# Second-level operand sums loaded one item ahead and a part of them split when formed, in a transformer block on one core

## The chip, the core and the metric

The kernel runs on one core of a Trainium2 chip. The metric is the device time of one execution in microseconds (us); of several runs the median is given. TensorE (PE) multiplies matrices, VectorE (DVE), ScalarE (ACT) and GpSimd (POOL) work elementwise, and SyncE (SP) issues every transfer between HBM and the on-chip memory (SBUF), in order. Each engine takes its instructions in the order of the program and stands at one whose inputs aren't there.

## The reference, cut to what matters

A block of 2048 tokens and width 1024: a normed attention with memory over four segments of 512 tokens, then a gated feed-forward with 3584 hidden columns, in float32.

```python
h = layernorm(x) * (1 + ca) + sa
x = x + ga * attention(h, wq, wk, wv, wo, beta)
h = layernorm(x) * (1 + cb) + sb
x = x + gb * ((gelu(h @ w_gate) * (h @ w_up)) @ w_down)
```

The change lies in the gate and up products `h @ w_gate` and `h @ w_up`, and in the places where this stage begins and ends.

## The kernel before, in words

**Products.** Every operand of the feed-forward's products is split into a high part (rounded, type fp32r) and a low part (the rest). A product is then three matmuls: high by high, low by high, high by low. The high part is a copy on ACT, the low part a subtraction on DVE, or on POOL in pieces of 256 columns.

**Two levels.** Gate and up are computed with a scheme of seven products for a 2 by 2 blocking instead of eight (products 1 to 7; 1 and 2 use the gate weights, 5 and 6 sums and differences of both weights, and 7, 3 and 4 are done later in `gate_up`). Products 1, 2, 5 and 6 are themselves cut by the same scheme a second time, so each has seven products r in the order ROUND = (1, 5, 6, 2, 7, 3, 4). An inner product is six matmuls of 128x128 by 128x512.

**Rounds.** `two(n)` runs for n = 0 to 27 (NJ = 14). Rounds 0 to 13 do products 1 and 2 for two chunks of hidden columns each, rounds 14 to 27 products 5 and 6. In a round the fourteen inner products (r, i) alternate between the two outer products i. After each inner product `ended` empties its PSUM bank (lines 1260 to 1289: ACT copies or DVE additions, L1270, L1274, L1276, L1280), and then `step()` advances every generator in the list `sides` by its rate. One such call is named a step here. `later(k, f)` runs f k steps on; stores are issued so. The bank of product 6 also takes 7 and 4, so 4 can't start until the addition for 7 (L1274) has read it; the bank of product 1 is copied into that bank by ACT first (L1260). y tiles, the results of the second outer product, have three buffers, which the base loads of rounds 14 and later (`base_load`, L1225) share.

**The operand from the tokens.** The activations' sums for products 1 and 2 are made by `a_early` and `a_first` while attention's output projections still run (`projections`, L783). The ones for 5 and 6 are made beside rounds 1 to 12 by `mixes`: first-level sums of the normed activations, eight items of two loads (h2_d to rm tiles, L964), three DVE sums and one POOL difference (L973), four stores to mix_d (L974); then second-level sums, four items of the same form (`a_mix_two`, L1012, to mix2_d). An item's loads stand at its beginning, four steps ahead of its first sum. `mixes` stands after the first four items until segment 3 of the tokens is normed (`norm_steps`, beside rounds 1 to 5). Their tiles have two buffers of each of two kinds (U, ra).

**The two entrances.** In round 13 each operand tile of products 1 and 2 comes free when its last product is done. `a_second` then fills it with the part for 5 or 6: 28 parts (seven r, two i, two halves c), six pairs loaded ahead (L1136, L1140), each split by `put_two` (ACT L1029, low half L933). In round 27 `a_last` does the same for the first-level operands of 7, 3 and 4, twelve loads (L1338) in `todo`, four ahead, each into a U or ra tile and split by `put_a` (ACT L936, low half L933). `gate_up(u)` then uses them; `cg_load` and `gu_load` bring its base sums and weights (L1362, L1368 to L1370). `b_two`, `b_one` and `b_part` prepare the weights' operands beside all of this (BB and B tiles; eight B buffers).

**Order.** All engines' orders in this stage are those of the program text: `manual_schedule` leaves nothing to a planner.

## Time and profile before

| | |
|---|---|
| median of 3 runs | 2688.2 us (2684.89 to 2689.12) |
| the profiled execution | 2689.39 us, span of its instructions 2687.5 us |
| PE busy | 2635.1 us, 98% of the span |
| DVE, ACT, POOL busy | 1742.5, 1382.0, 1043.0 us |
| mean granted TensorE clock | 0.997 |
| DMA | 617.83 MB, mean 230 GB/s |

The rows shown further on come from several views. In a row of the timeline stand the start in us from the span's beginning, the duration, engine, line, operation, output and inputs by the program's names, and the count of merged instructions; in brackets the idle time of the engine just before and what ended it. In a table of stages each row is a stretch of time with every engine's busy us. In a list of waits stand the waiter, whom it waited for, the total in us, how often, and the longest. SPq is the queue in which SP issues transfers. Where a helper records the instruction, its line is the helper's (L933: a sum or difference; L936 and L1029: a rounding copy).

The attention and its projections end at about 1116 us; rounds 0 to 27 of `two` run from there to 1686 us, `gate_up` to about 2166 us, the last product to the end.

### The profile page before, as it was taken

Reading aid. Unit: us, or ns where it says so; the run is one execution under the profiler, and the core shown is the slowest. Engines: PE = TensorE matmul, PEld = TensorE weight load, DVE = VectorE, ACT = ScalarE, POOL = GpSimd, SP = SyncE. Lnnn points to the kernel's source line nnn. Section 1 sums busy time; section 2 is a strip of 40 time slices with the busy share of each in tenths; the row PEclk is TensorE's granted clock in tenths of the full one; section 3 lists DMA queues with packets and bytes.
Section 4 is the critical chain, followed back from the end, with each engine's and each line's share of the span. In section 5 each row is a group of like instructions: output and inputs, shape, how many; then the busy total and the mean of one; then the engine's idle time right before and its main releaser. Section 6 shows DMA issues by size and latency. Waiting matters only on the chain.

```text
span 2687.5 us, 42440 instructions
## 1 busy us (share of the span) xinstructions
PE 2635.1 (98%) x13905; PEld 2188.8 (81%) x13905; DVE 1742.5 (65%) x3685; ACT 1382.0 (51%) x3163; POOL 1043.0 (39%) x1578
## 2 busy tenths in 40 slices
PE   7999999999999999999998999999999999999999
PEld 6788888888888788777876888788888888888887
DVE  7676656776676745776776555676767554574456
ACT  6778767776767724565564434433333333243323
POOL 4233334433333532334566675487877200000000
PEclk9999999999999999999999999999999999999999
DMA  7355444534443567487897778999999896885563
GB/s 266 107 156 159 112 140 134 153 103 138 138 128 101 169 207 263 143 292 265 306 315 266 276 270 289 345 363 375 360 359 365 302 325 222 274 296 196 189 207 123
DMA packets 284253, 617.83 MB, mean 230 GB/s; under 512 B 29056, under 2 KB 53632, under 8 KB 284032
## 3 DMA queue, kind: packets, MB, share of 16 engines
q1 hardware_dynamic: 284032, 615.13, 68.0%
q8 instruction: 109, 1.79, 0.3%
q14 instruction: 112, 0.92, 0.1%
HBM read 378.56 MB, written 186.12 MB: 210 GB/s over the span
## 4 chain that ended last, share of the span: by engine, by line
PE 88%; DMA 5%; DVE 4%; ACT 2%; issue 2%; POOL 0%; SPq 0%; DVEq 0%; ACTq 0%; POOLq 0%
PE y L1669 19%; PE f L1468 16%; PE kv L405 9%; PE pb L1248 6%; PE q L411 6%; PE y L783 6%; PE pa L1248 4%; PE pc L1248 4%; PE S L617 3%; PE T L705 3%; PE O L717 3%; PE kT L524 2%; PE vT L524 2%; DMA rm<-h_d 1%; PE num L673 1%
## 5 line engine op out<-in xcount | busy, mean ns | idle before, releaser
L1669 PE MATMUL y<-B,L 128*128 128x512 f32 x2352 | 533.8, 389 | 0.9 <-ACT L L936 0.6
L1669 PEld LDWEIGHTS y<-B,L 128*128 128x128 f32 x2352 | 441.4, 188 | 93.2 <-ACT L L936 1.0
L1468 PE MATMUL f<-A,B 128*128 128x512 f32 x2016 | 459.4, 390 | 3.9 <-ACT A L936 3.4
L1468 PEld LDWEIGHTS f<-A,B 128*128 128x128 f32 x2016 | 379.1, 188 | 84.0 <-ACT A L936 3.8
L621 ACT ACTIVATE sj<-sj,mm 128x384 f32<-128x384 f32 (+3 forms) x512 | 281.1, 552 | 39.9 <-DVE mm L619 39.4
L708 POOL TENSOR_SCALAR_AFFINE_SELECT pt<-pt 128x128 f32<-128x128 f32 x512 | 166.1, 346 | 332.6 <-ACT pt L707 324.5
L619 DVE CUSTOM_DVE_ANT_0 sj<-S,mask 128x384 f32<-128x384 f32 (+3 forms) x512 | 228.3, 488 | 96.5 <-PE S L617 70.2
L1248 PE MATMUL pb<-AA,BB 128*128 128x512 f32 x1008 | 250.8, 395 | 15.2 <-DVE AA L933 4.9
L707 ACT ACTIVATE pt<-T 128x256 f32<-128x256 f32 (+3 forms) x512 | 182.3, 443 | 132.3 <-PE T L705 126.0
L1248 PEld LDWEIGHTS pb<-AA,BB 128*128 128x128 f32 x1008 | 188.2, 189 | 63.0 <-DVE AA L933 8.1
L936 ACT ACTIVATE L<-X 128x512 fp32r<-128x512 f32 x168 | 105.7, 629 | 256.1 <-PE y L1669 165.4
L933 DVE TENSOR_TENSOR L<-X,L 128x512 fp32r<-128x512 f32 x168 | 115.9, 691 | 144.6 <-ACT L L936 144.5
L396 POOL TENSOR_TENSOR w<-r,w 128x256 fp32r<-128x256 f32 x180 | 133.8, 776 | 141.2 <-ACT w L390 141.2
L1495 ACT ACTIVATE g<-f 128x512 f32<-128x512 f32 x56 | 33.5, 598 | 285.0 <-PE f L1468 285.0
L405 PE MATMUL kv<-w,hha 128*128 128x256 f32 x896 | 173.8, 285 | 2.2 <-DVE vx L423 2.2
L1248 PE MATMUL pc<-AA,BB 128*128 128x512 f32 x672 | 163.3, 390 | 2.1 <-DVE AA L933 2.1
L1248 PE MATMUL pa<-AA,BB 128*128 128x512 f32 x672 | 164.0, 393 | 0.0
L1248 PEld LDWEIGHTS pc<-AA,BB 128*128 128x128 f32 x672 | 125.5, 188 | 30.0 <-DVE AA L933 3.9
L1248 PEld LDWEIGHTS pa<-AA,BB 128*128 128x128 f32 x672 | 127.4, 190 | 27.3 <-issue 0.5
L405 PEld LDWEIGHTS kv<-w,hha 128*128 128x128 f32 x896 | 143.9, 191 | 3.4 <-DVE vx L423 2.5
L933 DVE TENSOR_TENSOR BB<-t_a,BB 128x512 fp32r<-128x512 f32 x98 | 78.6, 802 | 86.3 <-ACT BB L936 86.2
L933 POOL TENSOR_TENSOR t_a<-g,t_a 128x256 f32<-128x256 f32 x112 | 95.6, 874 | 89.0 <-DVE BB L933 83.7
(295 smaller groups left out, 5442.4 us busy)
## 6 DMA issues: line engine op xcount, KB each, us to landing
B<-wc_d SPq DMA_DIRECT2D x112, 512.0 KB, 3.5
cg<-st_d SPq DMA_DIRECT2D x168, 256.0 KB, 6.3
st_d<-x SPq DMA_DIRECT2D x112, 256.0 KB, 2.7
st_d<-y SPq DMA_DIRECT2D x112, 256.0 KB, 3.1
hid_d<-g SPq DMA_DIRECT2D x56, 512.0 KB, 6.0
wc_d<-T SPq DMA_DIRECT2D x56, 512.0 KB, 4.6
X<-hid_d SPq DMA_DIRECT2D x112, 256.0 KB, 4.8
wr<-gd_d SPq DMA_DIRECT2D x84, 256.0 KB, 4.0
```

Source lines behind the costliest of these rows:

```text
L396: nc.gpsimd.tensor_sub(w[:, 1, c], r[:, c], f32(w[:, 0, c]))
L405: nc.tensor.matmul(ps, b[:, sl], w[:, a], start=(kt == 0 and a == 0 and b is hi), stop=(kt == KT - 1 and a == 1), **kw)
L411: nc.tensor.matmul(ps, w[:, a], b, start=(kt == 0 and a == 0 and b is hi), stop=(kt == KT - 1 and a == 1), **kw)
L619: nc.vector.tensor_tensor_reduce(out=sj[:, :nv], in0=ps[:, :nv], in1=mask[:, L - nv:], scale=-1.0, scalar=3.4e38, op0=ALU.add, op1=ALU.min ...
L621: nc.scalar.activation(sj[:, :nv], sj[:, :nv], AF.Exp, bias=mm[:, j, i:i + 1], scale=-1.0, accum_out=ll[:, i, j:j + 1])
L707: nc.scalar.activation(pt, ps[:, nn - n:nn], AF.Exp)
L708: nc.gpsimd.affine_select(pt[:, :P], pt[:, :P], pattern=[[1, P]], compare_op=ALU.is_ge, fill=0.0, base=0, channel_multiplier=-1)
L783: nc.tensor.matmul(ps, b[:, i * P:(i + 1) * P], w[:, a, g % 2], start=(g == 0 and a == 0 and b is hi), stop=(g == G - 1 and a == 1))
L933: f(*xs)
L1248: nc.tensor.matmul(ps, w[:, a, at:at + P], A["a", i, r, k][b], start=(r in (1, 5) and k == a == b == 0), stop=(k == 1 and a == 1), skip_gr ...
L1468: nc.tensor.matmul(ps, B[fc, i][:, a, kt * P:(kt + 1) * P], A[p, i, kt][b], start=False, stop=(kt == 3 and a == 1), skip_group_check=True)
L1669: nc.tensor.matmul(banks[t], ops[k][:, y, t * P:(t + 1) * P], B[slots[k]][:, x], start=(i not in (2, 4, 3) and j == 0 and x == 0 and y == ...
```

## The change

- `mixes` is one list of twelve items, each loaded one item ahead: at the end of the item before for the first five (and then eight steps before its first sum), behind the first sum of the item before for the others. Items alternate between U and ra tiles from the fifth on. First-level items form their sums in the order r = 5, 7, 6, 3 (before 5, 6, 7, 3), the one for 6 in place of an input.
- In the four second-level items, the parts for r = 5 and 7 (8 of the 28) are split at once: two ACT copies and two DVE subtractions, then stored as high and low to a new array hl_d (16 stores of 256 KB, in place of 8). `a_second` loads them straight into the operand tiles (16 loads of 256 KB) and splits only the other 20; two of these low halves (r = 6, c = 1) go to POOL.
- `base_load(14, 1)` stands behind product (2, 7) of round 13 instead of (2, 6).
- `a_last`: the last two of its twelve loads go into B tiles, issued in round 27 behind product (5, 7). `gu_load(2)` moves from the first to the second unit of `gate_up`.
- Before round 0, four parts of `a_first` are issued ahead of the five filling matmuls, and then one part a step instead of two. `a_first` forms one difference of each sum on POOL instead of DVE.
- `norm_steps`: segment 3 waits one step more before its transposes; segment 2 takes statistics and scaling one call earlier, the transposes one later (two calls a step there).

```diff
-                for _ in range(4):
+                for _ in range(5):
                     yield
                 turn(q, 0)
...
-        period, at_stat, at_scale, at_turn = (5, 5, 7, 10) if len(toks) > 4 else (4, 6, 8, 13)
+        period, at_stat, at_scale, at_turn = (5, 5, 7, 10) if len(toks) > 4 else (4, 5, 7, 14)
...
+            def one(p, kt):
                 r = []
                 for k in (kt, kt + 4):
-                    t = ra_tile(f"rm{p}_{k}") if p and kt % 2 else flat(pair_tile(f"rm{p}_{k}", "U"))
-                    nc.sync.dma_start(t, h2_d[k * P:(k + 1) * P, tok:tok + PASS])
+                    t = ra_tile(f"rm{p}_{k}") if p and kt % 2 == 0 else flat(pair_tile(f"rm{p}_{k}", "U"))
+                    nc.sync.dma_start(t, h2_d[k * P:(k + 1) * P, p * PASS:(p + 1) * PASS])
                     r.append(t)
...
+            items = [(one, p, kt) for p in range(2) for kt in range(4)] + [(two, i, c) for c in range(2) for i in PAIRS[1]]
+            homes = {0: items[0][0](*items[0][1:])}
...
+            for n, (f, x, y) in enumerate(items):
+                a11, a12, a21, a22 = homes[n]
+                if n < 5:
+                    for _ in range(8):
+                        yield
+                s1, s3 = c_tile(f"m1_{n}"), c_tile(f"m3_{n}")
+                split = f is two
+                for r, t, g, p_, q_ in ((5, s1, nc.vector.tensor_add, a21, a22), (7, s3, diff, a11, a21),
+                                        (6, a11, nc.vector.tensor_sub, s1, a11), (3, a12, nc.vector.tensor_sub, a12, a11)):
+                    g(t, p_, q_)
+                    k = (MIX.index(r) * 2 + y) * P
+                    if not split:
+                        later(3, lambda r=r, t=t, x=x, y=y: nc.sync.dma_start(mix_rows(x, r)[y * P:(y + 1) * P], t))
+                    elif r in (6, 3):
+                        later(3, lambda t=t, k=k, x=x: nc.sync.dma_start(mix2_d[x - 5][k:k + P], t))
                     yield
+                    if r == 5 and n > 3:
+                        ahead(n)
+                    elif r != 5 and (r != 6 or not split):
                         yield
+                if split:
+                    for r, t, h in ((5, s1, a22), (7, s3, a21)):
+                        nc.scalar.activation(h.bitcast(F32R), t, AF.Copy)
+                    yield
+                    for r, t, h in ((5, s1, a22), (7, s3, a21)):
+                        nc.vector.tensor_sub(t.bitcast(F32R), t, h)
+                        for q, src in enumerate((h, t)):
+                            k = (4 * (r == 7) + 2 * y + q) * P
+                            later(2, lambda src=src, k=k, x=x: nc.sync.dma_start(hl_d[x - 5][k:k + P], src))
+                        yield
+                else:
+                    yield
+                if n < 4:
+                    while n == 3 and not normed(3):
+                        yield
+                    ahead(n)
...
-                nc.vector.tensor_sub(s3, a11, a21)
+                diff(s3, a11, a21)
...
+                if r in (5, 7):
+                    for c in range(2):
+                        n = 8 * ROUND.index(r) + 4 * (i in (2, 6)) + 2 * c
+                        hl = A["a", i, r, c] = [a_tile(n + q, f"AA{i}_{r}_{c}_{q}") for q in range(2)]
+                        for q in range(2):
+                            k = (4 * (r == 7) + 2 * c + q) * P
+                            nc.sync.dma_start(f32(hl[q]), hl_d[i - 5][k:k + P])
+                    yield
+                    continue
                 for c in range(2):
-                    put_two(i, r, c, rs[q][c], nc.vector)
-                    if q and not c:
+                    put_two(i, r, c, rs[r, i][c], nc.gpsimd if r == 6 and c else nc.vector)
+                    if began and not c:
                         load()
...
-                if (second or n == NJ - 1) and (i, r) == (other, 6) and n + 1 < 2 * NJ:
+                if (i, r) == ((other, 6) if second else (other, 7)) and NJ - 1 <= n < 2 * NJ - 1:
                     base_load(n + 1, 1)
+                if n == 2 * NJ - 1 and (i, r) == (one, 7):
+                    ff["rest"]()
...
-                    t = (ra_tile if q % 4 > 1 else lambda n: pair_tile(n, "U"))(f"ra{p}_{i}_{b}")
+                    get = b_tile if q > 9 else ra_tile if q % 4 > 1 else lambda n: pair_tile(n, "U")
+                    t = f32(get(f"ra{p}_{i}_{b}"))
...
+            ff["rest"] = lambda: [load(q) for q in (10, 11)]
...
+        for _ in range(4):
+            next(ff["first"])
+        for e in sides:
+            if e[0] is ff["first"]:
+                e[1] = 1
         for q in range(5):
             nc.tensor.matmul(s_ps(f"full{q}"), B["a", 0, 1][:, 0, :P], A["a", 1, 1, 0][0], start=True, stop=True)
...
-                if fc + 2 < FC:
+                if 0 < fc < FC - 2:
                     gu_load(fc + 2)
+            if u == 1:
+                gu_load(2)
```

79 lines of the change are left out of this document (28 added, 51 removed).

## The prediction

> **What bounds the kernel now.** I read the page first, then the table of stages, then the list of who waited for whom, and last single rows at the gaps. The page says what can be won at all:
>
> ```profile
> span 2687.5 us, 42440 instructions
> PE 2635.1 (98%) x13905; PEld 2188.8 (81%) x13905; DVE 1742.5 (65%) x3685; ACT 1382.0 (51%) x3163; POOL 1043.0 (39%) x1578
> ```
>
> TensorE idles 52.4 us. The change adds and removes no matmul, so it can only touch this idle time and the clock. The table of stages (length, then busy us of PE, PEld, DVE, ACT, POOL, then granted clock, DMA share, GB/s) says where it lies:
>
> ```profile
> 0.00:100.00 100.00, 78.66 (x497) 67.24 (x498) 68.96 (x192) 67.28 (x135) 39.94 (x76) 0.97 0.62 211
> 1060.00:1116.00 56.00, 54.15 (x253) 44.12 (x252) 41.09 (x81) 21.25 (x39) 6.84 (x8) 1.00 0.51 165
> 1116.00:1140.00 24.00, 22.06 (x90) 17.76 (x89) 15.03 (x21) 14.22 (x25) 12.30 (x15) 0.93 0.32 110
> 1140.00:1303.00 163.00, 155.84 (x692) 125.74 (x691) 115.57 (x178) 92.19 (x171) 75.91 (x85) 1.00 0.83 279
> 1384.00:1437.00 53.00, 43.10 (x165) 30.23 (x164) 43.01 (x58) 31.76 (x61) 32.02 (x33) 0.98 0.89 318
> 1437.00:1686.00 249.00, 249.00 (x1094) 205.41 (x1093) 140.75 (x204) 102.31 (x180) 153.00 (x188) 1.00 0.78 277
> 1686.00:1708.00 22.00, 18.11 (x71) 13.90 (x70) 16.24 (x24) 11.80 (x21) 4.05 (x4) 0.92 1.05 405
> ```
>
> The opening's 21.3 us stay: nothing before 1060 us is edited. Five stages are in reach, by length less PE busy: end of the projections 1.85, round n=0 1.94, the rounds with the second-level sums (n=1 to 9) 7.16, the change from products 1 and 2 to 5 and 6 (n=13, 14) 9.90, the entrance to gate and up 3.89. Sum 24.7 us. A step (one product of six matmuls) is 249 / 1094 x 6 = 1.37 us, a round 19.1 us.
>
> Two of the gaps' groups (who waited for whom: us in total, times, longest) are needed below:
>
> ```profile
> PE tpb L269 <- ACT nb L248: 1.9, 2, 1.3
> PE tpc L269 <- ACT nc L248: 1.6, 2, 0.9
> ```
>
> The clock belongs to it. These rows show matmuls right behind a gap; the last number in brackets is PE's idle time:
>
> ```profile
> 1127.18 2.86 PE L1248 MATMUL pb<-AA,BB 128*128 128x512 f32 x6 [1.94 <-DVE x L1274]
> ...
> 1244.72 1.66 PE L1248 MATMUL pb<-AA,BB 128*128 128x512 f32 x6 [2.78 <-DVE y L1274]
> ...
> 1434.59 1.22 PE L1248 MATMUL pb<-AA,BB 128*128 128x512 f32 x2 [2.34 <-DVE AA L933]
> 1435.61 3.99 PE L1248 MATMUL pa<-AA,BB 128*128 128x512 f32 x12
> ...
> 1703.71 0.50 PE L1468 MATMUL f<-A,B 128*128 128x512 f32 x1 [3.38 <-ACT A L936]
> ```
>
> Six matmuls take 2.86 us at 1127 and 1.66 at 1244. The stages' clocks of 0.93 over 24 us and 0.92 over 22 us are 1.7 us of lost work each; the 14 matmuls from 1434.59 on end at 1439.60, 5.0 us instead of 14 x 0.228 = 3.2 and a tail, so I count 1.7 there too. So three gaps cost 5.1 us beyond their length, and the longer gap at 1244 cost nothing: length alone doesn't decide. The Trainium skill ("TensorE: Matmul & The Clock Gate", "What's actually happening") has the clock halve after an idle window of about 3.4 us, and the window runs free. The trace disagrees on the threshold: 1.94 and 2.34 us were enough. By the page only the third gap's 1.7 us would come back.
>
> In reach altogether: 24.7 + 5.1 = 29.8 us.
>
> **Part 1, end of the projections (1.85 us).** The transposes of segment 2 wait for the scaled rows: tpb's 1.9 us in two waits. Statistics and scaling move half a step up, the turn half a step down: 1.37 us more distance. I leave 0.3; gain 1.5 (0 to 1.9). The later turn delays the first sums by 0.7 us; the differences that go from DVE to POOL there are hidden, since POOL is busy 6.84 of those 56 us. If they weren't, DVE would wait for one pair of POOL instructions, 1.8 us by the 75.91 us that 85 of them take at 1140.
>
> **Part 2, round n=0 (1.94 + 1.7).** ACT's and DVE's rows:
>
> ```profile
> 1118.47 0.58 ACT L1260 ACTIVATE pb<-pa 128x512 f32<-128x512 f32 x1 [4.81 <-PE pa L1248]
> 1118.96 1.14 ACT L1029 ACTIVATE AA<-u 128x512 fp32r<-128x512 f32 x2
> ```
>
> ```profile
> 1119.62 1.29 DVE L933 TENSOR_TENSOR AA<-u,AA 128x512 fp32r<-128x512 f32 x2 [2.95 <-ACT AA L1029]
> 1126.45 0.69 DVE L1274 TENSOR_TENSOR x<-pb,x 128x512 f32<-128x512 f32 x1
> ```
>
> ACT stands 4.81 us at a bank copy that needs the first product, the splits queue behind it, DVE idles 2.95 us for them, and PE later waits 1.94 us for DVE's addition at 1126.45. Four parts issued ahead of the first product run in that hole: 4 x 0.57 = 2.3 us of ACT inside 4.81, and DVE's 2.95 us exceed the 1.94 missing. One part a step instead of two also puts fewer subtractions ahead of the addition. Gain 3.4 (0, if those tiles' memory comes free only with the last projection, to 3.6).
>
> **Part 3, sums one item ahead (7.16).** DVE's waits of these rounds, two of the seven rows, and the DMA issues (KB, median us to landing):
>
> ```profile
> DVE m L973 <- DMA rm<-h_d: 28.7, 7, 6.3
> ```
>
> ```profile
> 1150.82 0.69 DVE L973 TENSOR_TENSOR m<-rm,rm 128x512 f32<-128x512 f32 x1 [4.22 <-DMA rm<-h_d]
> ...
> 1242.77 0.69 DVE L973 TENSOR_TENSOR m<-rm,rm 128x512 f32<-128x512 f32 x1 [5.54 <-DMA rm<-h_d]
> ```
>
> ```profile
> rm<-h_d SPq DMA_DIRECT2D x16, 512.0 KB, 6.9
> mix_d<-rm SPq DMA_DIRECT2D x15, 256.0 KB, 5.3
> ```
>
> The load stands four steps (5.5 us) ahead of its first sum and lands in 6.9 us or more; DVE stands still, and the additions that empty PSUM queue behind it. The wait of 4.22 has no gap behind it, that of 5.54 the 2.78 at 1244. Of the 7.16 us, 1.6 are tpc, the transposes of segment 3, which get one step more (1.37 us against 0.9 at most); the other 5.5 are such additions that came late.
>
> The lead becomes eight steps for the first five items, seven or eight after: 9.6 to 10.9 us. But the tiles limit it: nine of the twelve loads enter a tile whose last store is issued in the same step or one before, and SP stands until that store lands, with the st_d stores and weight loads queued behind. Store 5.3 plus load 6.9 is 12.2 us, so waits of 1.3 to 2.6 us remain, below the 4.22 that cost nothing. DVE's third sum now follows POOL's difference by two steps, 2.7 us against two POOL instructions; a POOL that comes late would hold DVE there. The four split items add two ACT copies and two DVE subtractions each, into stages where ACT is busy 57% and DVE 71%.
>
> What grows is DMA. An eight-step item moves 2.1 MB in 10.9 us (192 GB/s), a nine-step split item 2.6 MB in 12.3 us (213), and a round's weights and st_d stores are 3.15 MB in 19.1 us (165): 357 to 378 GB/s. This stage's 279 GB/s at share 0.83 make 336 at full share; 405 were reached at 1686. So by the end the backlog lies between nothing and 33 us x 21 and 49 us x 42 GB/s, 2.8 MB or 8 us. I take half of that, which brings the last two items back to waits of 5 us and gaps near 1.5: 3.2 left, gain 4.0 (-3 to 7.2).
>
> **Part 4, n=13 and 14 (9.90 + 1.7).**
>
> ```profile
> L933 DVE TENSOR_TENSOR AA<-w,AA 128x512 fp32r<-128x512 f32 x28 | 23.0, 846 | 0.3 <-ACT AA L1029 0.3
> L1029 ACT ACTIVATE AA<-w 128x512 fp32r<-128x512 f32 x28 | 16.9, 622 | 0.0
> ```
>
> ```profile
> 1397.54 0.69 DVE L1280 TENSOR_TENSOR y<-pa,x 128x512 f32<-128x512 f32 x1 [3.25 <-DMA st_d<-y]
> ```
>
> DVE is the bound: 43.0 of 53.0 us busy, 10 in waits. PE needs 43.1 less 1.7 of slow clock, 41.4. The change takes 8 low halves off DVE and moves 2 to POOL: 10 x 0.846 = 8.5 us; 8 x 0.622 = 5.0 off ACT. The 3.25 us wait is for a y tile whose store hadn't landed: the base load ahead of it took the older tile. Moved four products down, it takes the younger one, and the wait goes. The sums also end earlier, since they no longer stand until segment 3 is normed, so the first six operand loads (3 MB) leave n=13. DVE then needs 53.0 - 8.5 - 3.2 = 41.3 against PE's 41.4, a tie, in which the order still costs something: I leave 3.5, gain 8.1 (3 to 11.6). Late next are the sixteen 256 KB loads straight into operand tiles. Those of r=7 are issued in n=14's first two steps and needed eight steps (10.9 us) on; a load of these rounds that meets DMA at its fullest stage lands in some 7 (the 6.9 above). If they were 3 us late, PE would wait 3; the range holds that.
>
> POOL's share of this is doubtful. Such an instruction on DVE takes 0.69 us at 1242.77 and 0.846 in the mean of these 28. By the Trainium skill ("SBUF — State Buffer", "SBUF: two separate sides") VectorE with two SBUF inputs and GpSimd lock each other out for a whole instruction. By it the two moved parts save DVE nothing, and part 4 would gain 1.7 us less.
>
> **Part 5, entrance to gate and up (3.89 + 1.7).** SP's issues and ACT's starts:
>
> ```profile
> 1690.12 0.37 SPq L1338 DMA_DIRECT2D ra<-mix_d  x1
> 1696.48 1.69 SPq L1338 DMA_DIRECT2D ra<-h_d  x2
> ```
>
> ```profile
> 1696.44 1.16 ACT L936 ACTIVATE A<-ra 128x512 fp32r<-128x512 f32 x2 [0.41 <-DMA ra<-mix_d]
> 1703.03 1.15 ACT L936 ACTIVATE A<-ra 128x512 fp32r<-128x512 f32 x2 [1.34 <-DMA ra<-h_d]
> ```
>
> The last two loads wait for tiles until 1696.48 and PE waits for them until 1703.71. In weight tiles they are issued near 1680 and land long before. Late next is the load before them, whose data come at 1696.44, 6.3 us after issue; it has the other 3.89 - 3.38 = 0.5 us of gap or part of it. The two early loads now stand ahead of it, 1.05 MB / 405 GB/s = 2.6 us at most, while the weights of fc=2 (1 MB, issued behind it anyway) move away from cg's loads. Left 1.3 without the slow clock; gain 4.3 (2.5 to 5.6).
>
> **Sum.** 1.5 + 3.4 + 4.0 + 8.1 + 4.3 = 21.3 us. The profiled execution took 2689.4 us around its span of 2687.5, 1.2 above the median of the runs, 2688.2. From 2689.4 it makes 2668.1; as a median, 2666.9: **2667**.
>
> **Rivals.**
>
> *The loads aren't really ahead.* Nine wait for a store, and the DMA queue fills: part 3 gives 0, part 4 only 4, the rest its 9.2. Gain 13, time 2675. For it: DMA shares of 0.83 to 1.05. Against: the lead still grows by 4.1 to 5.5 us, and the waits are 28.7 / 7 = 4.1 in the mean.
>
> *Only one slow clock goes.* If the slow clock at 1127 and 1434 hangs on more than the gap before it, as the free gap at 1244 suggests, 2 x 1.7 us stay: 2670. I give that 0.10 of the forecast's 0.60. It is also what the clock-gate rule above would make of the sum.
>
> *A new bound makes it slower.* In nine items SP stands still for a store, and the st_d stores queue behind it; then y tiles come free late, as at 1397.54, and DVE waits for them. If each cost what the worst cost (2.78) and half of these gaps drew the slow clock (1.7), part 3 would stand at 25 + 8 = 33 instead of 7.2 and undo the rest: 2688 + 26 - 17 = 2697. It decides from waits of 5.5 us on DVE per item, twice what I find.
>
> *Nothing moves.* What one stage wins, DMA takes back in the next: 2688. Against it: the five stages wait for different things.
>
> **How the numbers follow.** Forecast (gain 16 to 27) 0.60, loads not ahead (6 to 16) 0.24, nothing 0.08, slower 0.08. The measurement tells about 0.2%, 5.4 us. Range 2660 to 2681: below, all bounds but 1.6 us; above, the first rival with 6 us more. Faster 0.84, same 0.08, slower 0.08.
>
> **Right or wrong.** Right: no DVE wait above 3 us for rm or u; no L1274 gap above 1 us in n=0 to 12; L933 AA<-w 18 times on DVE near 1390; clock 1.00 at 1120, 1430 and 1700; A's last splits no longer behind ra<-h_d. Wrong: "DVE <- DMA st_d<-y" many times, SP long at mix_d or hl_d stores, PE waiting for a DMA at r=7 of n=14.

## The result, and the profile after

The changed kernel takes 2669.43 us (median of 8 runs), the kernel before 2685.82 us (8 runs beside them): a ratio of 0.9941, 95% interval 0.9923 to 0.996. The gain is 16.4 us where 21.3 were forecast; the forecast time was 2667. Seven of the eight runs lie between 2665.92 and 2672.39 us, one at 2684.13. The profiled execution took 2672.39 us. Its page:

```profile
span 2670.7 us, 42495 instructions
PE 2633.0 (99%) x13905; PEld 2193.0 (82%) x13905; DVE 1741.7 (65%) x3679; ACT 1383.3 (52%) x3163; POOL 1056.2 (40%) x1590
```

TensorE's idle time falls from 52.4 to 37.7 us. The stages (length, busy us of PE, PEld, DVE, ACT and POOL, granted clock, DMA share, GB/s), in the places that correspond to those of before:

```profile
0.00:100.00 100.00, 78.86 (x477) 67.93 (x477) 67.33 (x180) 64.37 (x120) 36.69 (x66) 0.91 0.60 204
1060.00:1117.00 57.00, 57.00 (x269) 47.49 (x269) 39.95 (x79) 23.49 (x44) 14.43 (x18) 1.00 0.53 168
1117.00:1141.00 24.00, 24.00 (x107) 19.62 (x106) 18.84 (x24) 15.90 (x28) 16.35 (x18) 1.00 0.47 145
1141.00:1304.00 163.00, 163.00 (x735) 134.79 (x734) 125.45 (x192) 101.75 (x184) 81.51 (x89) 1.00 0.89 303
1304.00:1336.00 32.00, 28.77 (x120) 21.87 (x119) 24.47 (x31) 13.95 (x27) 19.73 (x20) 1.00 0.95 348
1374.00:1420.00 46.00, 42.34 (x173) 33.10 (x172) 37.57 (x48) 29.31 (x56) 32.66 (x34) 0.93 0.97 352
1420.00:1670.00 250.00, 250.00 (x1100) 206.27 (x1099) 144.09 (x209) 103.47 (x182) 160.24 (x197) 1.00 0.80 285
1670.00:1692.00 22.00, 18.22 (x69) 12.95 (x68) 15.58 (x23) 10.43 (x20) 3.91 (x4) 0.96 1.05 404
```

From 1060 to 1304 us TensorE no longer idles. What is left lies at 1304, 1374 and 1670. The lengths below are differences between the starts of the first matmuls of each stage in the two profiled executions (84 matmuls make a round of `two`, 36 a unit of `gate_up`); "start" is all ahead of round 0's filling matmuls, without the end of the projections, which is counted by its idle time.

| stage | before, us | after, us | gain | forecast |
|---|---|---|---|---|
| end of the projections, idle | 1.85 | 0.00 | 1.9 | 1.5 |
| round 0 | 22.94 | 19.23 | 3.7 | 3.4 |
| rounds 1 to 12 | 242.35 | 237.49 | 4.9 | 4.0 |
| rounds 13 and 14 | 53.41 | 45.19 | 8.2 | 8.1 |
| rounds 15 to 27 | 250.40 | 249.32 | 1.1 | (the slow clock at 1434, in the 8.1) |
| first four units of gate and up | 38.81 | 40.01 | -1.2 | 4.3 |
| the rest | 962.64 | 961.57 | 1.1 | 0 |
| start | 1113.93 | 1116.73 | -2.8 | 0 |
| span | 2687.45 | 2670.68 | 16.8 | 21.3 |

Four of the five parts came out as forecast or better. The fifth failed, and the start, where nothing was changed, happened to be slower: the first row above has a granted clock of 0.91 where before had 0.97. In the clock's records the slow stretches of the start cost 8.5 us here and 3.4 before. (In after, L933 and L936 of before are L934 and L937, the sums are L992, L1029 is L1043, and L1248 and L1274 are L1274 and L1300.)

Who waited for whom between 1060 and 1712 us (total us, times, longest):

```profile
PE pb L1274 <- DMA AA<-hl_d: 3.4, 1, 3.4
PE f L1497 <- DVE A L934: 3.2, 5, 2.0
PE pb L1274 <- DVE y L1300: 1.1, 1, 1.1
PE pb L1274 <- DVE x L1300: 0.9, 2, 0.6
```

tpb and tpc are gone from the list, and in DVE's list the 28.7 us of waits for rm are gone. Three new losses have come.

**In rounds 9 and 10** (43.1 us together, 38.1 without a wait) DVE and SP wait as follows; the two rows below are one of DVE's and one of SP's:

```profile
DVE y L1306 <- DMA st_d<-y: 8.3, 3, 3.2
DVE m L992 <- DMA u<-mix_d: 3.1, 2, 1.7
```

```profile
SPq L1055 <- DMA hl_d<-u: 5.4, 3, 2.1
SPq L1055 <- DMA mix_d<-rm: 3.4, 2, 3.2
```

```profile
1308.80 0.69 DVE L1306 TENSOR_TENSOR y<-pa,x 128x512 f32<-128x512 f32 x1 [3.20 <-DMA st_d<-y]
```

```profile
1306.76 4.83 SPq L1055 DMA_DIRECT2D u<-mix_d  x2
```

SP stands for 4.83 us at two loads whose tiles still hold a part that is being stored (its waits name hl_d and mix_d); the stores of y behind them go late, and DVE waits for a free y tile. This is the mechanism of the rival "a new bound makes it slower", in three items at 5.0 us together instead of in nine at 33.

**In round 14** TensorE waits once, for a load straight into an operand tile, and the slow clock follows (twelve matmuls take 5.75 us; 2.88 elsewhere). The groups of DVE and POOL in this stage follow:

```profile
1401.79 2.88 PE L1274 MATMUL pa<-AA,BB 128*128 128x512 f32 x12
1408.09 5.75 PE L1274 MATMUL pb<-AA,BB 128*128 128x512 f32 x12 [3.42 <-DMA AA<-hl_d]
```

```profile
L934 DVE TENSOR_TENSOR AA<-w,AA 128x512 fp32r<-128x512 f32 x18 | 16.3, 924 | 0.0
L1296 DVE TENSOR_TENSOR y<-pa,y 128x512 f32<-128x512 f32 x1 | 0.7, 692 | 3.5 <-DMA y<-st_d 3.5
```

```profile
L934 POOL TENSOR_TENSOR AA<-w,AA 128x256 fp32r<-128x256 f32 x4 | 4.7, 1196 | 0.0
```

DVE makes 18 low halves instead of 28, as forecast. The late load is the one that the prediction named ("if they were 3 us late, PE would wait 3").

**At the entrance to gate and up** these are rows of SP, ACT and PE:

```profile
1663.11 1.79 SPq L1366 DMA_DIRECT2D ra<-h_d  x2
...
1667.01 2.31 SPq L1391 DMA_DIRECT2D cg<-st_d  x3
```

```profile
1675.00 0.60 ACT L1486 ACTIVATE f<-cg 128x512 f32<-128x512 f32 x1 [4.32 <-DMA cg<-st_d]
```

```profile
1687.54 1.19 DVE L1521 TENSOR_TENSOR g<-cg,cg 128x512 f32<-128x512 f32 x1
1688.65 1.81 DVE L934 TENSOR_TENSOR A<-ra,A 128x512 fp32r<-128x512 f32 x2
```

```profile
1689.91 6.44 PE L1497 MATMUL f<-A,B 128*128 128x512 f32 x20 [1.99 <-DVE A L934]
```

The two early loads are issued at 1663 us as meant, and the last splits no longer wait for them. But cg of the second unit stands behind them, and ACT stands 4.32 us for it with the splits queued behind. The same copy in the kernel before waited 1.76 us:

```profile
1690.15 1.19 ACT L1457 ACTIVATE f<-cg 128x512 f32<-128x512 f32 x2 [1.76 <-DMA cg<-st_d]
```

The difference, 2.56 us, is what the two loads were forecast to take (2.6). DVE then works from 1677 to 1690 us without a pause while TensorE waits for one split after another.

### The profile page after: what moved, and what is told of

It is laid out like the page before. It is cut to its first block, busy times and chain, and to the rows that moved or that the text cites. A ratio compares the mean times of both kernels' runs of the same rounds, so it can differ in the third digit from the quotient of the medians.

```text
span 2670.7 us, 42495 instructions
## 1 busy us (share of the span) xinstructions
PE 2633.0 (99%) x13905; PEld 2193.0 (82%) x13905; DVE 1741.7 (65%) x3679; ACT 1383.3 (52%) x3163; POOL 1056.2 (40%) x1590
## 4 chain that ended last, share of the span: by engine, by line
PE 93%; DMA 3%; DVE 2%; ACT 1%; issue 0%; POOL 0%; SPq 0%; DVEq 0%; ACTq 0%
PE y L1698 20%; PE f L1497 17%; PE kv L406 9%; PE pb L1274 8%; PE y L784 6%; PE q L412 6%; PE pa L1274 5%; PE pc L1274 5%; PE S L618 3%; PE T L706 3%; PE O L718 3%; PE kT L525 2%; PE vT L525 2%; PE num L674 1%; PE M L657 1%; PE kv L590 1%
## 5 line engine op out<-in xcount | busy, mean ns | idle before, releaser
L1274 PE MATMUL pb<-AA,BB 128*128 128x512 f32 x1008 | 248.5, 394 | 6.5 <-DMA AA<-hl_d 3.4
L937 ACT ACTIVATE L<-X 128x512 fp32r<-128x512 f32 x168 | 105.8, 630 | 257.3 <-PE y L1698 168.1
L1274 PEld LDWEIGHTS pb<-AA,BB 128*128 128x128 f32 x1008 | 189.1, 189 | 50.8 <-ACT AA L1043 3.8
L934 DVE TENSOR_TENSOR L<-X,L 128x512 fp32r<-128x512 f32 x168 | 115.9, 691 | 145.4 <-ACT L L937 145.0
L1274 PE MATMUL pc<-AA,BB 128*128 128x512 f32 x672 | 162.5, 390 | 0.4 <-DVE y L1300 0.4
L1274 PE MATMUL pa<-AA,BB 128*128 128x512 f32 x672 | 162.7, 390 | 0.0
L1274 PEld LDWEIGHTS pc<-AA,BB 128*128 128x128 f32 x672 | 126.1, 188 | 26.9 <-DVE y L1300 0.8
L1274 PEld LDWEIGHTS pa<-AA,BB 128*128 128x128 f32 x672 | 126.0, 188 | 26.7 <-issue 0.5
L934 DVE TENSOR_TENSOR BB<-t_a,BB 128x512 fp32r<-128x512 f32 x98 | 79.5, 812 | 85.6 <-ACT BB L937 85.5
L934 POOL TENSOR_TENSOR t_a<-g,t_a 128x256 f32<-128x256 f32 x112 | 98.3, 897 | 76.2 <-DVE BB L934 71.4
```

The source lines that it names most:

```text
L934: f(*xs)
L1274: nc.tensor.matmul(ps, w[:, a, at:at + P], A["a", i, r, k][b], start=(r in (1, 5) and k == a == b == 0), stop=(k == 1 and a == 1), skip_gr ...
```

## The experiments

The theory after this comparison: each part removed the wait it was aimed at; in rounds 9 and 10, in round 14 and at the entrance the DMA engines are full (share 0.95 to 1.05) and DVE has little to spare (busy 71 to 82%), so that the next wait stands close behind. The rivals: SP's order is at fault in each place (a load at another place would cost nothing), or the splits at their forming do nothing and the gain is DMA's. Each kernel below is the changed kernel with one edit and was run once, unless a ratio is given; the lengths of stages are taken as in the table above. A single time also holds what the start happened to take (1109.9 to 1116.7 us in these kernels), so the stage and not the total decides. A stage scatters too: kernels whose code for it is the same take 44.8 to 46.5 us for rounds 13 and 14, and 38.6 to 40.3 us for the first four units. About half of the second spread is the slow clock; without what it costs the first four units take 38.2 to 39.0 us.

**No load ahead.** Each item loads at its beginning, as in the kernel before; the rest of the change stays.

```diff
-            homes = {0: items[0][0](*items[0][1:])}
+            homes = {}
...
+                ahead(n - 1)
...
-                if n < 5:
-                    for _ in range(8):
-                        yield
+                for _ in range(4):
+                    yield
...
-                    if r == 5 and n > 3:
-                        ahead(n)
-                    elif r != 5 and (r != 6 or not split):
+                    if r != 5 and (r != 6 or not split):
                         yield
...
-                    ahead(n)
```

> The changed kernel, but every item of the sums is loaded at its own beginning, four steps ahead of its first sum. Rounds 1 to 12 took 242.4 us before and 237.5 in the changed kernel. Theory: loading ahead is what gained the 4.9 us; DVE again waits for rm loads, 20 us or more in total, and rounds 1 to 12 take 241 to 243 us, with the y tiles' waits of rounds 9 and 10 (8.3 us on DVE) smaller. Rival: the gain came from the transposes' extra step and the moved stores; rounds 1 to 12 stay at 236 to 239 us.

Rounds 1 to 12 take 242.49 us (before 242.35), and DVE's waits are back:

```profile
DVE m L992 <- DMA rm<-h_d: 30.0, 8, 7.3
```

The waits are back in full, so loading ahead is what removed them. The stage's length tells it less cleanly: 3.4 of the 242.49 us are a slow clock at 1170 us that the kernel before didn't draw there, and without it 239.1 are left, 1.6 above the changed kernel in the same rounds and 2.8 to 3.6 above most of its variants below. Rounds 13 and 14 take 54.06 us, all of part 4's gain lost, with a wait for hl_d of 6.2 us; that this comes of sums that end later is likely and wasn't shown apart. Rounds 9 and 10 take 38.5 us here, so their loss comes with the loads ahead. Part 4 needs part 3.

**None split when formed.** All 28 parts are split in rounds 13 and 14.

```diff
-                split = f is two
+                split = False
...
-                    if not split:
+                    if f is one:
...
-                    elif r in (6, 3):
+                    else:
...
-            whole = [e for e in todo if e[0] not in (5, 7)]
+            whole = list(todo)
...
-                if r in (5, 7):
+                if r in ():
```

> The changed kernel, but no part is split when formed: all 28 are stored whole, loaded whole and split in rounds 13 and 14 as before (8 more low halves on DVE, 8 more copies on ACT, no hl_d). Theory (DVE is the bound of rounds 13 and 14): they take 48 to 51 us instead of 45.2 (53.4 before, when the y wait of 3.3 us came on top); rounds 9 and 10 lose their excess of 5 us in part, since 16 stores become 8. Rival: the moved base load alone was worth it; rounds 13 and 14 take 42 us or less, since the wait for hl_d is gone too.

Rounds 13 and 14 take 52.17 us, 7.0 more than with the splits (48 to 51 were expected). DVE is busy 50.7 of 55 us there at a DMA share of 0.83, and TensorE waits for DVE and, in this stage, for no transfer:

```profile
PE pb L1274 <- DVE AA L934: 5.1, 7, 2.0
PE pc L1274 <- DVE AA L934: 2.2, 4, 0.8
```

Rounds 1 to 12 take 240.72 us here: one gap of 4.0 us in round 9 drew 3.4 us of slow clock, and DVE's waits for u rise from 3.1 to 7.3 us. An item without the splits is shorter, so that its loads are less far ahead. Rounds 9 and 10 take 42.0 us without the slow clock: the gain expected there can't be told from the scatter (41.3 to 43.1 us).

**Only r = 5 split when formed.** r = 7 is stored whole and split in round 14: half the volume in its loads, four more low halves for DVE.

```diff
-                    elif r in (6, 3):
+                    elif r in (6, 7, 3):
...
-                    for r, t, h in ((5, s1, a22), (7, s3, a21)):
+                    for r, t, h in ((5, s1, a22),):
...
-            whole = [e for e in todo if e[0] not in (5, 7)]
+            whole = [e for e in todo if e[0] != 5]
...
-                if r in (5, 7):
+                if r == 5:
```

> The changed kernel, but only the parts for r = 5 are split when formed (4 of 28); those for r = 7 are stored whole, loaded whole and split in round 14. Against the changed kernel this takes 1 MB of stores and 1 MB of loads off DMA and puts 4 low halves (3.4 us) back on DVE. Rounds 13 and 14 took 45.2 us with 8 parts, 52.2 with none. Theory (two bounds, DMA with 8 parts, DVE with none): the wait for hl_d goes, and the two rounds take 42 to 46 us. Rival (DVE alone bounds them, the wait for hl_d being an accident of the order): halfway, 48 to 49 us.

44.95 us, against 45.19: no difference in length. The wait for hl_d is gone, and others have come in its place:

```profile
PE pb L1275 <- DVE y L1297: 2.5, 1, 2.5
PE pb L1275 <- DVE AA L934: 1.9, 3, 0.8
PE pc L1275 <- DVE AA L934: 0.7, 2, 0.5
```

Eight parts or four cost the same by different ways. With eight it is one gap of 3.42 us and 3.4 us of slow clock behind it; with four it is six waits for DVE, 5.2 us together, and no slow clock at all.

**r = 7 loaded ahead of r = 2.** The loads from hl_d are issued earlier in round 14.

```diff
-            todo = [(r, i) for r in ROUND for i in PAIRS[1]]
+            todo = [(r, i) for r in (1, 5, 6, 7, 2, 3, 4) for i in PAIRS[1]]
```

> The changed kernel, but the parts for r = 7 are taken up ahead of those for r = 2, so their eight direct loads are issued four steps earlier. Rounds 13 and 14 took 45.2 us in the changed kernel, 38.1 of it matmuls; 3.4 of the rest is PE waiting for AA<-hl_d, and 3.4 the slow clock behind it. Theory (order): the loads came late because they stood behind other transfers in SP's queue; issued earlier they are there in time, rounds 13 and 14 take 39 to 40 us and the whole 5 to 6 us less. Rival (volume): DMA moves as much as it can in these rounds; another transfer is late instead (operands of r = 3 and 4, the y base loads, weights), and the two rounds stay at 44 to 46 us.

47.47 us, more than either forecast. The wait for hl_d falls to 0.9 us, but a base load is now late: SP stands 5.4 us at it until a y tile is stored. DVE waits for this load in front of the addition that TensorE needs, and TensorE waits longer than in the changed kernel:

```profile
1409.58 0.69 DVE L1296 TENSOR_TENSOR y<-pa,y 128x512 f32<-128x512 f32 x1 [5.48 <-DMA y<-st_d]
```

```profile
1411.61 4.72 PE L1274 MATMUL pb<-AA,BB 128*128 128x512 f32 x12 [4.52 <-DVE x L1300]
```

SP's order is not the fault by itself: with these loads put ahead, another transfer came late.

**The base load at its old place.** The bases of products 1 to 6 are all issued at (other, 6), as in the kernel before.

```diff
-                if (i, r) == ((other, 6) if second else (other, 7)) and NJ - 1 <= n < 2 * NJ - 1:
+                if (i, r) == (other, 6) and NJ - 1 <= n < 2 * NJ - 1:
```

> The changed kernel, but the first y base load stands again behind product (2,6) of round 13. Theory: y of round 13 gets the younger tile again, DVE waits 2 to 4 us for DMA st_d<-y in that round, and rounds 13 and 14 take 47 to 50 us instead of 45.2. Rival: with DMA as the bound this wait lies beside another; the two rounds stay at 44 to 46 us.

44.66 us, where 47 to 50 were expected: nothing is lost by the old place. DVE's wait for st_d<-y there is 1.2 us, not the 3.25 of the kernel before, so the move of four products, which the prediction credited with those 3.2 us, did little; the total of 2663.18 us comes from the start (1110.6 us) and from an entrance without the slow clock.

**The last two loads later.** `ff["rest"]` behind the second load of cg instead of ahead of it.

```diff
-                if n == 2 * NJ - 1 and (i, r) == (one, 7):
-                    ff["rest"]()
                 if n == 2 * NJ - 1 and (i, r) in ((one, 2), (one, 3)):
                     cg_load(int(r == 3), (0, 2, 1))
+                if n == 2 * NJ - 1 and (i, r) == (one, 3):
+                    ff["rest"]()
```

> The changed kernel, but the two early loads of the last operands are issued behind the base sums of unit 1 (product (5,3) of round 27) instead of ahead of them. The first four units of gate and up took 40.0 us in the changed kernel and 38.8 before, 32.7 of it matmuls. Theory: ahead of the base sums the two loads hold up ACT, which stands 4.3 us at the bank copy of unit 1 with all later splits behind it; behind them ACT waits under 2.5 us, and four units take 34 to 36 us. Rival (DVE): the last splits are bound by DVE's own work, which ran without a pause for 13 us; the four units stay at 39 to 40 us.

40.67 us in the first four units, no gain. ACT's wait for cg falls from 4.32 to 1.77 us, as the theory had it, and another comes behind it:

```profile
1674.18 1.15 ACT L937 ACTIVATE A<-ra 128x512 fp32r<-128x512 f32 x2 [3.80 <-DMA ra<-mix_d]
```

**The last two loads behind load 9.** Of the twelve loads (counted from 0; the expectations call number 9 the tenth or the ninth), these are now the last in the queue as in the kernel before, but still in B tiles.

```diff
+                if q == 6:
+                    ff["rest"]()
                 while ("a", 6, ROUND[q // 2]) not in done:
```

> The changed kernel, but the two early loads of the last operands are issued behind the load of the tenth pair (the one that lands last), still into weight tiles. Issued ahead of the base sums (changed kernel) or behind them, the first four units of gate and up took 40.0 and 40.7 us, and what stands next in the queue came late each time. Theory (volume): DMA is full here and hands out what was asked first; with the two loads last, the pairs ahead land 2.6 us sooner, PE's waits for DVE's splits shrink from 2.9 to 3.2 us to under 1.5, the two loads themselves land some 6 us before they did in the kernel before, and four units take 35 to 37 us. Rival (DVE): the splits' own work bounds the stage; four units stay at 38.6 us or more.

38.25 us: 1.8 less than in the changed kernel, 0.6 less than before, all three with the same 1.7 us of slow clock. TensorE's waits for DVE's splits fall from 3.2 to 0.9 us, as the theory had it, but one of 2.1 us for ACT's copies comes in their place. ACT waits for cg four times, 2.5 us at the longest; 5.6 us are still lost.

**Some low halves by GpSimd.** The edit above, and of the last twelve splits every second low half on POOL, which idles there.

```diff
-                    put_a(p, i, 2 * b + k, rs[q][:, k], nc.vector)
+                    put_a(p, i, 2 * b + k, rs[q][:, k], nc.gpsimd if q > 5 and k else nc.vector)
```

> The load of the rest stands behind the ninth load, as in e5_rest_behind, and of the splits of the gate/up operands for the second half of the rows (a_last's numbers 6 to 11) every second low part is made by GpSimd, which the profile shows idle from 1660 to 1685, instead of VectorE: six of 0.68 us leave VectorE. The theory that VectorE bounds the entrance (it runs without a pause for over 7 us while TensorE waits for A): the first four units take 38.25 us in e5_rest_behind, 32.6 without a wait, and fall to 34 to 36.5 here. The rival that ScalarE's high parts and the loads before them bound it: they stay at 37.5 to 39. The rival that GpSimd's two instructions of 256 columns (0.70 us each alone, about 1.2 beside VectorE) make each low come later than VectorE would have: 39 us or more, with TensorE's waits at L1497 naming POOL.

38.59 us, which by itself would speak for the first rival. But TensorE's waits for A are 1.4 us for ACT, 0.2 for DVE and 0.2 for POOL, and the granted clock tells the rest: 6.8 us at half speed where the edit above had 3.4. Less the lost halves (3.4 and 1.7) it is 35.2 against 36.5. What is left of the waits is ACT's, as the first rival had it. POOL is no free helper: beside it DVE's subtractions take up to 1.22 us instead of 0.68.

```profile
1674.20 1.22 DVE L934 TENSOR_TENSOR B<-ru,B 128x512 fp32r<-128x512 f32 x1
```

**The next item's load three steps later** in the second-level items, so that SP comes when the tiles are free.

```diff
-                    if r == 5 and n > 3:
+                    if r == (6 if split else 5) and n > 3:
```

> In the second-level items the loads for the next item are issued after the sum r=6 instead of after r=5, three steps later; everything else is the changed kernel. The theory of SP's place: rounds 9 and 10 of the products lose time (43.1 us for the two in the changed kernel, 41.3 to 43.1 in its variants, 38.1 without any wait) because SP stands at these loads (12.6 us in 7 waits at L1055) until earlier stores have left their buffers, and the stores of y behind them go late, so that VectorE waits for st_d<-y (8.3 us in 3). Three steps later the buffers are free when SP comes, SP's standing falls below 7 us, the waits for st_d<-y below 4 us, and the two rounds take 39 to 40.5 us. The rival, volume: the DMA engines are full in this stretch and the stores would be late in any order; then the two rounds stay at 41 us or more, and the waits for st_d<-y stay above 5 us. A second rival: the loads now come late for the sums, VectorE's waits for u<-mix_d rise from 3.1 us to 8 or more, and the mixes end later, so that rounds 13 and 14 lose more than their 45.2 us.

The theory's first half holds: SP's waits at L1055 fall from 12.6 us (1280 to 1340 us) to 6.6 in the same stretch, and DVE's for st_d<-y are gone from the list. The two rounds still take 41.3 us, and DVE now waits for the loads:

```profile
DVE m L992 <- DMA u<-mix_d: 7.6, 4, 3.2
```

In the changed kernel it was 3.1 us of these and 8.3 for st_d<-y, 11.4 in all. So the second rival holds in part: the loads come late for the sums, but rounds 13 and 14 stay at 45.20 us. Round 10 costs 22.3 us in this kernel and 22.2 to 23.7 in every other that loads ahead and splits early; 41.3 us for the two rounds is also what three of those take.

**Round 0 without the early parts.** The four parts of `a_first` are not issued ahead, and two go in a step again.

```diff
-        for _ in range(4):
-            next(ff["first"])
-        for e in sides:
-            if e[0] is ff["first"]:
-                e[1] = 1
```

> The changed kernel, but no part is issued ahead of the five filling matmuls, and two parts go out a step as before. Round 0 took 22.9 us before and 19.2 in the changed kernel. Theory: the four parts ahead of the bank copy are the whole gain of round 0; it takes 22 to 23 us again, with a wait of PE for x of about 2 us and the slow clock behind it. Rival: the difference that POOL now forms in place of DVE gave part of it; round 0 takes 20 to 21.5 us.

Round 0 takes 21.34 us instead of 19.2, so the edit is worth 2.1 us. That lies in the range of the rival, but PE's wait for x is 2.0 us as in the kernel before (1.9); only the slow clock behind it is missing. The run, though, took 2686.91 us: 16.3 of them go in the fifth unit of `gate_up` (the expectation below calls it the fourth, and the multiplication a subtraction), over 550 us behind the edit. DVE's and POOL's rows there:

```profile
1704.17 0.69 DVE L1520 TENSOR_TENSOR cg<-f,cg 128x512 f32<-128x512 f32 x1 [2.03 <-PE f L1497]
1704.89 19.67 DVE L1521 TENSOR_TENSOR g<-cg,cg 128x512 f32<-128x512 f32 x1
```

```profile
1713.10 1.40 POOL L934 TENSOR_TENSOR t<-rw,t 128x256 f32<-128x256 f32 x2
...
1717.18 5.47 POOL L1436 TENSOR_TENSOR rw<-rw,gbb 128x256 f32<-128x256 f32 x8
```

One multiplication of 0.69 us lasted 19.67, while POOL worked without a pause at 0.70 us an instruction, and TensorE ran dry. It ended at 1724.56, half a microsecond behind the last of POOL's instructions (1724.02). To see whether the edit brings this about, the same kernel was run again:

> The kernel of e8_start_back once more. There, one subtraction of VectorE (0.69 us elsewhere) lasted 19.67 us in the fourth unit of gate/up while GpSimd worked without a pause, and took 16.3 us from that run at a place that the edit doesn't touch. The theory that this was chance: the long instruction is not there again in the profile, the fourth unit takes 8.2 us, and the run takes 2 us more than the changed kernel (round 0 is 21.3 us instead of 19.2), 2665 to 2676, a ratio to the kernel before of 0.994 to 0.997. The rival that the edit brings it about: 2680 us or more, a ratio above 0.998, with the long instruction in the profile.

2670.54 us (median of 4 runs), ratio 0.9949, interval 0.9934 to 0.9965; the long instruction isn't in the profile, and the highest of the four times is 2671.74 us. So the edit alone doesn't bring it about. The same place here, where both engines go on:

```profile
1705.29 1.07 DVE L1521 TENSOR_TENSOR g<-cg,cg 128x512 f32<-128x512 f32 x1
```

```profile
1705.09 1.88 POOL L934 TENSOR_TENSOR ru<-ru 128x256 f32<-128x256 f32 x2
```

Round 0 took 21.30 us, with the gap of the kernel before but without its slow clock:

```profile
1126.76 1.66 PE L1274 MATMUL pb<-AA,BB 128*128 128x512 f32 x6 [1.91 <-DVE x L1300]
```

**Three edits together.** The base load at its old place, the last two loads behind load 9, and the low halves by GpSimd.

```diff
-                if (i, r) == ((other, 6) if second else (other, 7)) and NJ - 1 <= n < 2 * NJ - 1:
+                if (i, r) == (other, 6) and NJ - 1 <= n < 2 * NJ - 1:
...
+                if q == 6:
+                    ff["rest"]()
...
-                    put_a(p, i, 2 * b + k, rs[q][:, k], nc.vector)
+                    put_a(p, i, 2 * b + k, rs[q][:, k], nc.gpsimd if q > 5 and k else nc.vector)
```

> Three edits that each looked no worse than the changed kernel, together: the bases of products 1 to 6 loaded at one place in all second rounds (e7_base_back), the load of the rest behind the ninth load, and every second low part of the last gate/up splits by GpSimd (e10_pool_lows). The theory that the three remaining losses have causes of their own and add: rounds 1 to 12 take 235.6 us, rounds 13 and 14 44.7, the first four units 36 to 38.6, so the kernel comes out 2 to 4 us below the changed kernel, at a ratio to the kernel before of 0.991 to 0.993 (0.9941 for the changed kernel). The rival that these edits only pass one wait on to another, and that the differences of single looks (2663 to 2672 us) are where the slow clock happened to fall: no gain that can be told from the changed kernel, a ratio of 0.993 to 0.996.

2665.51 us (median of 5 runs), ratio 0.9931, interval 0.9918 to 0.9943. Rounds 1 to 12 take 236.29 us, 13 and 14 44.58, the first four units 37.09. The first four units are 2.9 us shorter than in the changed kernel, which agrees with the theory; in the total the two intervals overlap, so that a gain over the changed kernel isn't shown. TensorE's waits at the entrance:

```profile
PE f L1497 <- ACT A L937: 1.6, 1, 1.6
PE f L1497 <- DVE A L934: 0.2, 1, 0.2
```

## Why the prediction was right, and where it wasn't

**Part 1** (forecast 1.5): right; no idle time is left at the end of the projections, 1.9 us, and the waits for the transposes are gone. No run took this part back alone.

**Part 2** (3.4): right in total, 3.7, and in mechanism. Undone, it gives 21.3 us, so 2.1 are the edit's own; the other 1.6 are the slow clock of the kernel before, which the undone edit did not bring back in two profiles. That term hung on luck, on where a gap of the same length fell in the clock's windows (last section).

**Part 3** (4.0): the mechanism is shown by the kernel without loads ahead. The size was on the cautious side: 4.9 us in this profile, 6.0 to 6.8 in nine of the other kernels that load ahead and 4.2 in a tenth, of which the new places of the norming steps and of the sums have a share that wasn't taken apart. The 3.2 us that the prediction left "in the last two items" are the 3.2 to 5.0 us of rounds 9 and 10. It gave a DMA backlog as their cause; what is seen first is SP's standing and the y tiles, but when SP was freed the loads came late. Both lie on one path. The kernel that splits nothing early has 2 MB less to store and gained nothing there that can be told, but its loads stand less far ahead, so which of the two would have to go stays open.

**Part 4** (8.1): 8.2 in the two rounds, and 1.1 of slow clock behind them, 9.3 in all. That DVE bounded the stage is shown by the kernel that splits nothing early (52.17 us). Of the 45.19 us that are left, 3.4 are a new slow clock. One term was wrong: "Moved four products down, it takes the younger one, and the wait goes" earned nothing that can be seen, as the base load at its old place does as well. The doubt about POOL stays open: its low halves of 256 columns took 1196 ns each, and DVE's mean for one rose from 846 to 924 ns, 18 x 0.078 = 1.4 us, about the 1.7 that the prediction's doubt takes off. That the two moved parts did this isn't shown: POOL as a whole was busy 60% of this stage before and 71% after. The gain stood all the same. The remainder is not DVE's order, as forecast, but the late load of r = 7 and the slow clock behind it, which the prediction named as next.

**Part 5** (4.3): wrong; it lost 1.2. The step that failed is "The two early loads now stand ahead of it, 1.05 MB / 405 GB/s = 2.6 us at most ... Left 1.3 without the slow clock". The 2.6 us came, but in another place: it counted one load behind the two, and not cg of the second unit, for which ACT stands 4.32 us instead of 1.76 with the splits in its queue. Nor did it ask whether DVE had room: its 16.24 us of 22 at 1686 looked like slack, but with the loads there it worked 13 us on end and TensorE still waited for splits. With the two loads behind load 9 the stage takes 38.25 us, and with low halves on POOL as well 37.09 and 38.59: no order of these loads that was run won back the remaining 5.6 us. A full clock would not have saved the forecast either: five other kernels with this entrance escaped the slow clock and took 38.6 to 39.0 us, where 34.5 were forecast. The move of `gu_load(2)` was in every kernel and wasn't taken apart.

**The rest.** The start took 2.8 us more in the profile of after; its length varies by 6.9 us among the changed kernel and its variants, and by 2.4 without what the slow clock costs there, so this is no effect of an edit.

**The rivals.** "The loads aren't really ahead" and "nothing moves" are refuted by rounds 1 to 12. "Only one slow clock goes" came near in time (2670) for another reason: all three slow clocks went from their old places, and two new ones came, at 1408 and 1690. "A new bound" came true in three items only. Of the prediction's own signs, the one for PE's gaps in rounds 0 to 12 was just missed (one of 1.1 us), and the clock was full at 1120 and 1430 but not at the entrance. Two of its signs of being wrong came: SP long at hl_d and mix_d stores, and PE waiting for a DMA at r = 7.

## What to carry to other kernels

When a load is moved ahead in a queue whose DMA share is near 1, write down every transfer that it passes, who needs each, and what is queued behind that reader on its in-order engine; the gain is what remains after that. Where two resources are both near full, taking work from one buys only the distance to the other, so undo each part alone to see which of them holds the stage. Judge an edit worth a few microseconds by the length of its own stage, and take out what the slow clock cost there before comparing, since both the stage and the total hold what the clock happened to do.

## What the runs showed of the hardware

**The slow clock goes by windows, not by gaps.** Every stretch of half clock in these profiles up to 2600 us lasts 3.41 us or a whole multiple of it, and within one profile the stretches start whole multiples of 3.413 us apart: in the kernel before at 38.43, 1127.29, 1434.49 and 1704.14 us, which are 319, 90 and 79 of them. So the profile can be cut into such windows. The first two rows below are the window with the 1.94 us gap of round 0 and the one behind it; the next two hold the 2.78 us gap at 1244 (busy us as in the table of stages, the granted clock third from the end):

```profile
1123.87:1127.29 3.42, 1.48 (x8) 0.90 (x6) 3.02 (x6) 2.15 (x4) 0.89 (x2) 1.00 0.20 77
1127.29:1130.70 3.41, 3.41 (x9) 2.67 (x10) 0.44 (x1) 0.62 (x2) 3.41 (x6) 0.50 0.72 191
1239.93:1243.35 3.42, 2.01 (x9) 1.32 (x8) 0.58 (x1) 0.00 (x0) 0.00 (x0) 1.00 0.85 315
1243.35:1246.76 3.41, 2.04 (x9) 1.70 (x10) 3.38 (x6) 0.83 (x2) 3.22 (x4) 1.00 0.27 100
```

The gap of 1.94 us lies in one window, which is idle for 1.94 us, and the next window is slow. The longer one is split into 1.4 and 1.4, and none follows. In the repeat of round 0 above the gap of 1.91 us is split as well, into 0.66 and 1.25:

```profile
1122.09:1125.51 3.42, 2.76 (x12) 1.90 (x11) 3.01 (x5) 2.40 (x5) 1.07 (x1) 1.00 0.02 5
1125.51:1128.92 3.41, 2.16 (x9) 1.80 (x10) 1.79 (x3) 0.86 (x2) 2.94 (x5) 1.00 0.63 179
```

Between 1050 and 1720 us of the fourteen profiles, all 24 windows at full clock in which TensorE idled 1.8 us or more were followed by a slow one, two of nine with 1.6 to 1.8, and none with less. The idle time of a window adds up: at the entrance of the three edits together a gap of 1.61 us alone would not have reached 1.8, but its window (from 1677.50) holds another of 0.22.

```profile
1679.73 0.50 PE L1497 MATMUL f<-A,B 128*128 128x512 f32 x1 [1.61 <-ACT A L937]
```

Where the windows fall differs from run to run, which is the luck in it; a gap of 3.4 us or more has half a window's idle time wherever it falls. The Trainium skill ("TensorE: Matmul & The Clock Gate", "What's actually happening") has a free-running window of about 3.4 us, and these windows agree. That a whole window must be idle does not agree: a little over half of one was enough. (Earlier, beside attention, two slow stretches came behind windows with 1.4 us of idle time, so the half isn't the whole rule.)

**GpSimd can hold VectorE up for long.** In the run told above a VectorE instruction with two SBUF inputs stood for 19.67 us while GpSimd finished some 28 instructions; in the repeat the two took turns, VectorE at 1.07 us and GpSimd at 0.94 instead of 0.69 and 0.70. So long a hold was seen once in fourteen profiles; the next longest such instruction of VectorE behind 1100 us takes 1.30 us. The Trainium skill ("SBUF — State Buffer", "SBUF: two separate sides") says that the two lock each other out for a whole instruction. That agrees with 1.30 us, which is less than one instruction of each on end (0.69 + 0.70). That the lock can go to one side for many instructions on end is not in the rule; it is read here from one case, in which VectorE came free as GpSimd stopped, and what decides it stays open. The one run of the changed kernel at 2684.13 us, 14.7 above the median, has no profile, so that it can't be said whether it met the same.
